# Last tile's first product by seven half products in six single PSUM banks, with its weight sums made earlier

## The chip, the cores and the metric

The kernel runs on one core of a Trainium2 chip. TensorE multiplies matrices, VectorE and ScalarE work on elements, GpSimd does a few set-up steps, SyncE (SP) and ScalarE issue transfers. TensorE writes to PSUM (eight banks of 128 x 512 floats), and the other engines read results from there. The metric is the time of one execution on the device, in microseconds (us).

## The reference, cut to what matters

An attention-like recurrence (rwkv6) gives x, of 3072 tokens by 384; what is changed here lies behind it, in the two-layer network:

```
h = x @ w_in                 # 3072 x 384  by  384 x 2048
g = 0.5 * h * (1 + erf(h / sqrt(2)))
out = g @ w_out              # 3072 x 2048 by 2048 x 384
```

All is float32.

## The kernel before, in words

The tokens are cut into eight tiles of T = 384 (`NX` = 8; two tiles make one sequence). `attention(x, 0)` is a generator that yields in slots; it fills `xT`, tile x's tokens laid out with the model width on the 128 partitions in three parts of 128 (j = 0, 1, 2). `mlp(x)` is a generator for the network of one tile. A main loop steps through `mlp(x - 1)` and at written-out steps (`place`, `place_next`) calls the next slot of `attention(x)`, so the program order on each engine is that of this loop; there is no other scheduler, and each engine runs its instructions in that order. The last tile, `mlp(NX - 1)`, has no attention beside it (L958).

In `mlp`, h is made in 16 strips of 128 of the hidden width (L747 to L754): three products, one for each part j, of 384 columns, accumulated in one PSUM bank `h_ps` (tag "mm", two buffers), and then a Gelu on ScalarE into g. Then g @ w_out: the tile's 384 tokens are three blocks of 128. Blocks 0 and 1 go by seven products of halves (L796 to L838, the method of Strassen and Winograd: the hidden width in two halves of 8 strips, the output width in two halves of `HM` = 192), with sums of g in `s1`, `s2`, `s3` (L763 to L766, on VectorE), sums of w_out in `sums` (`w_sums`, made once), and partial results `p1`, `u2`, `u3`. `product` (L769) issues the eight products of one half. Block 2 of an odd tile is kept (`alone`) and goes with block 2 of the next tile (`waits`, `ends`), but the last tile's block 2 stands alone: 16 plain products of 384 columns (L877 to L893), after the seven, then a copy by VectorE (L891) and a store. Stores are issued on SP's queue (L740). The sums of g are made in the last two of the 16 strips (L758 to L766).

Tile 6, the one before, is an `ends` tile: its steps 16 to 22 are its seven products of g, beside the last slots of `attention(7)`. At step 18 these are the products with v (L595) and the chain of states on VectorE (L610); at step 20 L636 and the fences (L648); at step 21 L674 and the copies of `xT` by ScalarE (L697, L700), with six small transfers for the rest of `xT` (L704). Steps 23 to 27 are five more products, of the kept block pair (L855 to L876), with L856, L859, L862, L864, L867, L870 and L874 as their readers and sums. PSUM is split in a pool `ps`: two single banks of tag "mm", and three pairs of banks of tag "d" for the attention.

The names p, s1 and so on appear in the profile without their numbers; `rkw` is the pair of input buffers (`bufs`), parts of which are used again for `alone`, `p1_alone` and others.

Of the kernel before, what the change touches and what calls it, by code (L numbers as in the profile page):

```python
# [10 lines left out]
F32 = mybir.dt.float32  # L11
# [33 lines left out]
def kernel(  # L45
# [40 lines left out]
    cv = ctx.enter_context(tc.tile_pool(name="cv", bufs=HALFWAY))  # L86
    gp = ctx.enter_context(tc.tile_pool(name="gp", bufs=4))
    ps = ctx.enter_context(tc.tile_pool(name="ps", bufs=1, space=PSUM))
    ctx.enter_context(tc.manual_schedule(engines=None))

    half = [slice(0, 64), slice(64, 128)]
# [94 lines left out]

    def keep_warm(n, elsewhere=False):
        if elsewhere:
            t = ps.tile([128, 2, BANK], F32, name="warm", tag="d", bufs=3)[:, 0]
        else:  # L190
            t = ps.tile([128, BANK], F32, name="warm", tag="mm", bufs=2)
        for _ in range(n):
            nc.tensor.matmul(t, lhsT=zeros[:, 0:128], rhs=zeros, start=True, stop=True)  # L193
# [123 lines left out]
    def attention(x, unit):  # L317
# [78 lines left out]
            yield  # L396

        def products(bs, right, width):
            d = ps.tile([128, 2, BANK], F32, name="d", tag="d", bufs=3)
            n = 0  # L400
            for b in bs:
                for i in range(NI):
                    for g in range(2):
                        for p in range(2):
                            nc.tensor.matmul(d[half[p], g, n * width:(n + 1) * width],  # L405
                                             lhsT=kc[half[g], b, i, p], rhs=right(half[g], b, i, p),
                                             start=True, stop=True)
                    n += 1
            return d[:, :, 0:n * width]
# [64 lines left out]
        def quarters():  # L474
# [26 lines left out]
            yield  # L501
            for h in QUARTERS:
                m, r4, t4, s0, s1, s2 = views(h)
                banks = [ps.tile([128, 2, BANK], F32, name="d", tag="d", bufs=3) for _ in range(0, np_ * NI, 4)]
                if h == FINE:

                    n_b = np_ * NI
                    fine_ps = [banks[-1][:, g, 6 * C:6 * C + FINE * n_b] for g in range(2)]
                    for a in range(FINE):
                        for g in range(2):  # L510
                            nc.tensor.matmul(fine_ps[g][:, a * n_b:], lhsT=places[half[g], a], rhs=fine_sb[half[g], 0:FINE - a, a],  # L511
                                             start=(a == 0), stop=True, skip_group_check=True)
                ds = []
                for n, d in zip(range(0, np_ * NI, 4), banks):
                    for i in range(4):
                        for g in range(2):
                            for p in range(2):
                                nc.tensor.matmul(d[half[p], g, i * 3 * C // 2:(i + 1) * 3 * C // 2],  # L518
                                                 lhsT=kc[half[g], (n + i) // NI, (n + i) % NI, p],
                                                 rhs=rx[half[g], 2 * (n + i) + p], start=True, stop=True)  # L520
                    ds.append(d[:, :, 0:4 * 3 * C // 2].rearrange("p g (n x) -> p g n x", n=4))
                last = h == QUARTERS[-1]

                z = r4[:, :, :, 1:, :].rearrange("p n m b j -> p n m (b j)")
                nc.vector.tensor_mul(z, s0, t4[:, :, :, 0:1].to_broadcast(z.shape))
                if not last:
                    plain(4 * h)
                k4 = k.rearrange("p (n four j) -> p n four j", four=4, j=h)
                z = k4[:, :, 0:2, :].rearrange("p n b j -> p n (b j)")
                t2 = tot[2 * h].rearrange("p (n two) -> p n two", two=2)  # L530
                nc.vector.tensor_mul(z, z, t2[:, :, 1:2].to_broadcast(z.shape))  # L531
                z = k4.rearrange("p n (b two) j -> p n b two j", two=2)[:, :, :, 0, :]
                tz = t4.rearrange("p n m (b two) -> p (n m) b two", two=2)[:, :, :, 1:2]
                nc.vector.tensor_mul(z, z, tz.to_broadcast(z.shape))
                if not last:
                    lay_out(4 * h)
                else:
                    blocks_of_k()
                    yield
                    for move in moves[NC_SP:]:  # L540
                        move_block(nc.scalar, *move)
                for n, d in enumerate(ds):
                    an = at[:, :, 4 * n:4 * n + 4].rearrange("p g n (m x) -> p g n m x", m=m)
                    o = 0
                    for a in range(3):
                        w_q = (3 - a) * C // 4
                        mask = quarter[h][a].rearrange("p (m x) -> p m x", m=m).unsqueeze(1).unsqueeze(1)
                        data = d[:, :, :, o:o + w_q].rearrange("p g n (m x) -> p g n m x", m=m)
                        nc.vector.copy_predicated(out=an[:, :, :, :, (a + 1) * h:], mask=mask.to_broadcast(data.shape), data=data)  # L549
                        o += w_q  # L550
                if h == FINE:
                    mask = fine_mask.rearrange("p (m b) -> p m b", b=FINE).unsqueeze(1)
                    for g in range(2):
                        data = fine_ps[g].rearrange("p (b n) -> p n b", n=n_b)
                        data = data.unsqueeze(2).to_broadcast([128, n_b, C // FINE, FINE])
                        nc.vector.copy_predicated(out=at[:, g].rearrange("p n (m b) -> p n m b", b=FINE),  # L556
                                                  mask=mask.to_broadcast(data.shape), data=data)
                yield
# [4 lines left out]
        if x < 2:  # L563
            kts = []
            for b in range(np_):
                kt_ps = ps.tile([128, 2, BANK], F32, name="kt_ps", tag="d", bufs=3)
                for i in range(NI):
                    o = (i % N3) * 128
                    nc.tensor.transpose(kt_ps[:, i // N3, o:o + 128], k[:, (b * NI + i) * 128:(b * NI + i + 1) * 128], ident)  # L569
# [18 lines left out]

        kvs = []
        for b in range(np_):  # L590
            kv_ps = ps.tile([128, 2, BANK], F32, name="kv_ps", tag="d", bufs=3)
            for i in range(NI):
                for p in range(2):
                    for g in range(2):
                        nc.tensor.matmul(kv_ps[half[g], p, i * D:(i + 1) * D], lhsT=k_t(b, i, p, g),  # L595
                                         rhs=vs(b, i, g)[half[p], 0:D], start=True, stop=True)
            kvs.append(kv_ps[:, :, 0:NI * D].rearrange("p c (q i e) -> p q i c e", q=Q, e=D))
# [27 lines left out]
        def inside():  # L625

            for b in range(np_):
                if split:
                    y = [ps.tile([128, BANK], F32, name="y_ps", tag="mm", bufs=2) for _ in range(2)]
                else:  # L630
                    y_ps = ps.tile([128, 2, BANK], F32, name="y_ps", tag="d", bufs=3)
                    y = [y_ps[:, c] for c in range(2)]
                for i in range(NI):
                    for p in range(2):
# [82 lines left out]
    def w_sums():  # L717
# [3 lines left out]
        for i, (x, y) in enumerate((((0, 1), (0, 0)), ((1, 1), 0), ((1, 1), (0, 1)), ((1, 0), 1))):  # L721
            for k in range(2):
                ks = slice(k * FG, (k + 1) * FG)
                nc.vector.tensor_sub(sums[i][:, ks], w_quarter(*x, k), sums[y][:, ks] if isinstance(y, int) else w_quarter(*y, k))
                yield

    def mlp(x):


# [12 lines left out]
        def new_sums(tag):  # L742
            return cv.tile([128, FG, 128], F32, name="s", tag=tag)

        s1, s2, s3 = [], [], []
        for n, group in enumerate((0, 2, 1, 3) if halves else range(4)):
            gs[group] = gp.tile([128, FG, T], F32, name="g")  # L747
            for f in range(group * FG, (group + 1) * FG):
                h_ps = ps.tile([128, BANK], F32, name="h_ps", tag="mm", bufs=2)[:, 0:T]
# [6 lines left out]
                    nc.scalar.activation(out=alone[:, f], in_=h_ps[:, t:], func=AF.Gelu)  # L756

                if halves and n == 3 and f % FG >= FG - 2:  # L758
                    k = f % FG - FG + 2
                    for s, tag in ((s1, "f"), (s2, "e")):  # L760
                        s.append(new_sums(tag))
                    s3.append(s3_sb[0][:, k * FG:(k + 1) * FG])
                    a00, a10, a11 = (gs[g][:, :, a:a + 128] for g, a in ((k, 0), (k, 128), (k + 2, 128)))  # L763
                    nc.vector.tensor_add(s1[k], a10, a11)  # L764
                    nc.vector.tensor_sub(s2[k], s1[k], a00)
                    nc.vector.tensor_sub(s3[k], a00, a10)  # L766
                yield

        def product(o, lhs, rhs, start=False):  # L769
# [21 lines left out]

        def two_rows():
            return [wk.tile([128, DM], F32, name="o_sb", bufs=2) for _ in range(2)]


        if halves:  # L796
# [54 lines left out]
        elif ends:  # L851
# [22 lines left out]
            nc.vector.tensor_add(o_sb[0][:, 0:HM], o1, u2)  # L874
            store(row0 - T + 256, o_sb[0][:, 0:HM], HM)
            yield  # L876
        else:  # L877

            if halves:
                psum()  # L880
            for blocks in ((2,),) if halves else ((0, 1), (2,)):
                o_ps = [ps.tile([128, BANK], F32, name="o_ps", tag="mm", bufs=2)[:, 0:DM] for _ in blocks]
                for f in range(NF):
                    for i, o in zip(blocks, o_ps):
                        nc.tensor.matmul(o, lhsT=block(i, f // HF, f % HF), rhs=w_out_sb[:, f, :],  # L885
                                         start=(f == 0), stop=(f == NF - 1))
                    if (not halves or f % 4 == 3) and f < NF - 1:
                        yield
                for i, o in zip(blocks, o_ps):
                    o_sb = wk.tile([128, DM], F32, name="o_sb", bufs=2)  # L890
# [39 lines left out]
    for x in range(1, NX):  # L930
# [8 lines left out]
        for step, _ in enumerate(mlp(x - 1)):  # L939
# [12 lines left out]
            while place_next and place_next[0] <= step:  # L952
                place_next.pop(0)
                next(following, None)
        for _ in slots:
            pass
        slots = following
# [62 lines left out]
```

## Time and profile before

| | us |
|---|---|
| median of four runs (607.61 to 608.85) | 607.95 |
| the profiled execution | 607.84 |
| its span, first to last instruction | 605.3 |
| TensorE busy in the span | 589.6 (97%) |
| VectorE busy | 446.7 (74%) |
| ScalarE busy | 173.4 (29%) |
| h of all tiles, 768 records of 384 columns | 254.2 |
| granted clock of TensorE, mean | 1.000 |

The profile's rows give start and length in us, then engine, line of the kernel, operation, what it writes and reads, shape, and how many instructions were merged into the row (x16). PE is TensorE's products, PEld its weight loads, DVE VectorE, ACT ScalarE, SPq the issue of transfers by SP. Brackets give the idle time of the engine before the row, and what ended it. [...]rows of TensorE overlap by some 0.16 us; the distance between starts is what a product takes. The records' granted clock is 1.0 throughout. The chain that ended last is TensorE for 93% of the span.

### The profile page before, as it was taken

The numbers are of one execution on the slowest core, as the hardware profiler recorded it, in microseconds if no ns is written. First come the engines' busy times: TensorE is split into PE (matmuls) and PEld (weight loads), VectorE is DVE, ScalarE is ACT, GpSimd is POOL, SyncE is SP. The second block draws the span as 40 slices with busy tenths as digits, with TensorE's granted clock in tenths as the row PEclk, the third lists the DMA queues.
The fourth block names the chain that finished last, engine by engine and source line by source line (L and its number), as shares of the span: only waits on it lengthen the run. The fifth ranks groups of instructions, "written<-read, shape, count | busy, mean of one in ns | idle before, by whom it ended". The sixth has DMA issues, their size and how long they took to land.

```text
span 605.3 us, 15833 instructions
## 1 busy us (share of the span) xinstructions
PE 589.6 (97%) x6913; PEld 445.0 (74%) x6928; DVE 446.7 (74%) x837; ACT 173.4 (29%) x389; POOL 8.4 (1%) x24
## 2 busy tenths in 40 slices
PE   8769999999999999999999999999999999999997
PEld 4556666656698669986699568986699568995694
DVE  7979999998876978488885988579885988621120
ACT  2346376023222322213222332213222232112200
POOL 3100000000000000000000000000000000000000
PEclk9999999999999999999999999999999999999999
DMA  5767358112041305203042304203052002010001
GB/s 198 233 221 228 107 158 301 34 35 75 15 118 59 92 2 110 73 21 93 1 111 79 92 2 95 86 21 93 2 111 72 8 1 40 23 37 0 1 1 39
DMA packets 50564, 46.70 MB, mean 77 GB/s; under 512 B 31680, under 2 KB 35904, under 8 KB 50496
## 3 DMA queue, kind: packets, MB, share of 16 engines
q1 hardware_dynamic: 33152, 29.31, 15.9%
q10 hardware_dynamic: 17344, 16.39, 10.0%
q8 instruction: 54, 0.88, 0.6%
q14 instruction: 14, 0.11, 0.1%
HBM read 36.24 MB, written 4.72 MB: 68 GB/s over the span
## 4 chain that ended last, share of the span: by engine, by line
PE 93%; DVE 5%; issue 1%; ACT 0%; DVEq 0%
PE h_ps L751 40%; PE o_ps L771 31%; PE o_ps L885 7%; PE d L518 4%; PE d L405 2%; PE kv_ps L595 2%; PE y_ps L674 2%; PE y_ps L636 2%; DVE rkw L440 2%; PE warm L193 1%; DVE a_sb L450 1%; PE d L511 1%; DVE a_sb L416 1%; PE kt_ps L569 0%; DVE e L309 0%
## 5 line engine op out<-in xcount | busy, mean ns | idle before, releaser
L751 PE MATMUL h_ps<-xT,w_in_sb 128*128 128x384 f32 x768 | 254.2, 489 | 0.0
L751 PEld LDWEIGHTS h_ps<-xT,w_in_sb 128*128 128x128 f32 x768 | 144.1, 190 | 97.0 <-ACT xT L681 0.4
L754 ACT ACTIVATE g<-h_ps 128x384 f32<-128x384 f32 (+1 forms) x128 | 57.2, 449 | 196.4 <-PE h_ps L751 196.4
L771 PE MATMUL o_ps<-t,s 128*128 128x192 f32 x480 | 81.9, 329 | 0.0
L771 PEld LDWEIGHTS o_ps<-t,s 128*128 128x128 f32 x480 | 77.8, 190 | 0.7
L549 DVE COPY_PREDICATED a_sb<-quarter,d 128x384 f32<-128x384 uint8 (+2 forms) x108 | 45.1, 439 | 2.5
L885 PE MATMUL o_ps<-w_out_sb,g 128*128 128x384 f32 x128 | 42.7, 490 | 0.0
L771 PE MATMUL o_ps<-w_out_sb,g 128*128 128x192 f32 x224 | 38.7, 326 | 0.0
L771 PEld LDWEIGHTS o_ps<-w_out_sb,g 128*128 128x128 f32 x224 | 37.0, 190 | 1.9
L885 PEld LDWEIGHTS o_ps<-w_out_sb,g 128*128 128x128 f32 x128 | 23.8, 190 | 16.3 <-DVE o_sb L891 0.6
L610 DVE SCALAR_TENSOR_TENSOR st<-st,tot_sb,kv_ps 128x48 f32<-128x48 f32 x160 | 29.0, 259 | 4.1 <-PE kv_ps L595 4.1
L764 DVE TENSOR_TENSOR s<-g 128x512 f32<-128x512 f32 x14 | 9.4, 671 | 29.1 <-ACT g L754 29.1
L771 PE MATMUL o_ps<-w_out_sb,s 128*128 128x192 f32 x160 | 28.3, 330 | 0.0
L405 PEld LDWEIGHTS d<-rkw 64*64 64x64 f32 x1152 | 18.8, 136 | 12.8 <-DVE rkw L440 7.4
L771 PE MATMUL o_ps<-t,g 128*128 128x192 f32 x160 | 27.6, 326 | 0.0
L342 DVE TRANSPOSE_TENSOR_REDUCE rkw<-kx 128x48 f32<-128x1536 f32 (+3 forms) x24 | 26.8, 1157 | 0.2
L518 PEld LDWEIGHTS d<-kx,rkw 64*64 64x64 f32 x1152 | 24.3, 133 | 3.4 <-DVE a_sb L556 1.6
L518 PE MATMUL d<-kx,rkw 64*64 64x96 f32 x1152 | 26.5, 245 | 0.0
L771 PEld LDWEIGHTS o_ps<-t,g 128*128 128x128 f32 x160 | 26.3, 190 | 0.0
L771 PEld LDWEIGHTS o_ps<-w_out_sb,s 128*128 128x128 f32 x160 | 25.9, 190 | 0.4
L405 PE MATMUL d<-rkw 64*64 64x64 f32 (+1 forms) x1152 | 21.3, 223 | 5.1 <-DVE rkw L440 2.9
L531 DVE TENSOR_TENSOR rkw<-rkw,tot_sb 128x768 f32<-128x768 f32 x12 | 11.5, 959 | 17.3 <-PE d L518 17.3
(116 smaller groups left out, 632.9 us busy)
## 6 DMA issues: line engine op xcount, KB each, us to landing
rkw<-in_rkw_dram ACTq DMA_DIRECT2D x45, 256.0 KB, 2.8
raw<-in_w_out_dram SPq DMA_DIRECT2D x8, 768.0 KB, 4.4
out_dram<-o_sb SPq DMA_DIRECT2D x21, 192.0 KB, 1.9
raw<-in_w_in_dram SPq DMA_DIRECT2D x5, 768.0 KB, 5.9
v_in<-in_v_dram ACTq DMA_DIRECT2D x5, 584.0 KB, 3.6
raw<-in_w_in_dram SPq DMA_DIRECT2D x9, 256.0 KB, 3.4
rkw<-in_rkw_dram SPq DMA_DIRECT2D x8, 288.0 KB, 3.4
rkw<-in_rkw_dram SPq DMA_DIRECT2D x9, 256.0 KB, 7.5
```

What stands on the lines that cost most here:

```text
L342: nc.vector.tensor_reduce(out=fine_sb[:, e, 0:n].rearrange("p a n -> p (a n)"), in_=kx[:, o:o + n * n_m].rearrange("p (m j) -> p m j", j=3 ...
L405: nc.tensor.matmul(d[half[p], g, n * width:(n + 1) * width], lhsT=kc[half[g], b, i, p], rhs=right(half[g], b, i, p), start=True, stop=True)
L440: nc.vector.tensor_mul(rk, rk, tt)
L518: nc.tensor.matmul(d[half[p], g, i * 3 * C // 2:(i + 1) * 3 * C // 2], lhsT=kc[half[g], (n + i) // NI, (n + i) % NI, p], rhs=rx[half[g], 2 ...
L549: nc.vector.copy_predicated(out=an[:, :, :, :, (a + 1) * h:], mask=mask.to_broadcast(data.shape), data=data)
L595: nc.tensor.matmul(kv_ps[half[g], p, i * D:(i + 1) * D], lhsT=k_t(b, i, p, g), rhs=vs(b, i, g)[half[p], 0:D], start=True, stop=True)
L610: nc.vector.scalar_tensor_tensor(out=stq[:, q, c], in0=stq[:, q, c - 1] if c else b4[:, q, NC - 1], scalar=totq[:, q, c:c + 1], in1=kvs[q ...
L636: nc.tensor.matmul(y[p][half[g ^ swap(b)], i * C:(i + 1) * C], lhsT=vs(b, i, g)[half[p]], rhs=at[half[p], g, b * NI + i, :], start=(i == 0 ...
L751: nc.tensor.matmul(h_ps, lhsT=w_in_sb[:, f // FI, j, f % FI * 128:(f % FI + 1) * 128], rhs=xT[:, j, :], start=(j == 0), stop=(j == NJ - 1))
L754: nc.scalar.activation(out=gs[group][:, f % FG, 0:t], in_=h_ps[:, 0:t], func=AF.Gelu)
L771: nc.tensor.matmul(o, lhsT=lhs(j), rhs=rhs(j), start=start and j == 0, stop=(j == HF - 1), skip_group_check=True)
L885: nc.tensor.matmul(o, lhsT=block(i, f // HF, f % HF), rhs=w_out_sb[:, f, :], start=(f == 0), stop=(f == NF - 1))
```

## The change: what it does, and the diff

For the last tile, h is made by seven products of halves over the first two parts of the model width (j = 0, 1), the two halves a = 0, 1 of the hidden width (strips f and f + 8), and the two halves b of the tokens (192 each). The third part (j = 2) is added by plain products of 192 columns. So there are eight blocks, one for each f, of 11 products of 192 columns, in six single banks in place of the two: p1 (in b_1), S2 T2 (b_6), S3 T3 (b_7), S1 T1 (b_5), the rest of h00 (b_1 again, added to it), w11 T4 and its third part (b_4), a third part alone (b_0), S4 x11 and a third part (b_5 again, added). VectorE adds them to u2, u3, u5, c21, c22, c12; ScalarE copies p1 and takes four Gelus of 192 columns a block, one from b_1 and three from the sums in SBUF. The Gelu of c12 is issued in the next block behind the copy of p1. In the profile the six banks b_1, b_6, b_7, b_5, b_4, b_0 are named b0 to b5, in that order.

`h_sums` makes the sums of w_in (S1 to S4, eight instructions of 128 x 512) and of xT (T1 to T4, four of 128 x 192) on VectorE, at steps 18, 22 (two parts) and 25 of the tile before, into buffers that are no longer read: parts of `rkw`, `kx`, `tot_sb` and a new `v_in`. The sums of g (`of_g`) are spread over the blocks 4 to 6 and behind the last. The third token block's 16 products go ahead of the seven products of g, with the copy on ScalarE; L891 and its store at the end are gone for the last tile. The pairs of banks get a pool of their own (`pd`), which is closed before the six banks are opened; every other use of tag "d" only changes its pool's name.

```diff
+    pairs_of_banks = ctx.enter_context(ExitStack())
+    pd = pairs_of_banks.enter_context(tc.tile_pool(name="pd", bufs=3, space=PSUM))
...
+    def h_sums():
+        n = DF // 2
+        rest = io.tile([128, v.shape[2]], F32, name="v_in")
+        for z in (bufs[0][:, 0:n], rest[:, 0:n], kx[:, 0:n], bufs[1][:, ALL:ALL + n]):
+            in_s.append(z.rearrange("p (i c) -> p i c", c=WI))
...
+        for i in range(4):
+            for k in range(2):
+                if i == 0:
+                    nc.vector.tensor_add(s(1, k), w(1, 0, k), w(1, 1, k))
+                elif i == 1:
+                    nc.vector.tensor_sub(s(2, k), s(1, k), w(0, 0, k))
+                elif i == 2:
+                    nc.vector.tensor_sub(s(3, k), w(0, 0, k), w(1, 0, k))
+                else:
+                    nc.vector.tensor_sub(s(4, k), w(0, 1, k), s(2, k))
+            if i < 3:
+                yield
...
+        nc.vector.tensor_sub(in_t[0], x01, x00)
+        nc.vector.tensor_sub(in_t[1], x11, in_t[0])
+        nc.vector.tensor_sub(in_t[2], x11, x01)
+        nc.vector.tensor_sub(in_t[3], x10, in_t[1])
+        yield
...
+        def of_g(k):
...
+            nc.vector.tensor_add(s1[k], a10, a11)
+            yield
+            nc.vector.tensor_sub(s2[k], s1[k], a00)
+            yield
+            nc.vector.tensor_sub(s3[k], a00, a10)
+            yield
+
+        def h_halves():
+            pairs_of_banks.close()
+            pb = ctx.enter_context(tc.tile_pool(name="pb", bufs=1, space=PSUM))
+            b_1, b_6, b_7, b_5, b_4, b_0 = (pb.tile([128, BANK], F32, name=f"b{i}")[:, 0:HT] for i in range(6))
...
+            for f in range(HF):
...
+                multiply(b_1, (w(0, 0), x00))
+                nc.scalar.copy(out=p1, in_=b_1)
+                for z in late:
+                    gelu(*z)
+                multiply(b_6, (s(2), in_t[1]))
+                nc.vector.tensor_add(u2, b_6, p1)
+                multiply(b_7, (s(3), in_t[2]))
+                nc.vector.tensor_add(u3, b_7, u2)
+                multiply(b_5, (s(1), in_t[0]))
+                nc.vector.tensor_add(u5, b_5, u3)
+                multiply(b_1, (w(0, 1), x10), (w(0, 2), last[0]), start=False)
+                gelu(0, 0, b_1)
+                multiply(b_4, (w(1, 1), in_t[3]), (w(1, 2), last[0]))
+                nc.vector.tensor_add(c21, b_4, u3)
+                gelu(1, 0, c21)
+                multiply(b_0, (w(1, 2), last[1]))
+                nc.vector.tensor_add(c22, b_0, u5)
+                gelu(1, 1, c22)
+                multiply(b_5, (s(4), x11), (w(0, 2), last[1]), start=False)
+                nc.vector.tensor_add(c12, b_5, u2)
+
+                late = [(0, 1, c12, f)]
+                next(more, None)
+                if f % FG == FG - 1:
+                    more = of_g(k)
+            for z in late:
+                gelu(*z)
+            for _ in more:
+                pass
...
+        final = x == NX - 1
+        if final:
+            h_halves()
+        for n, group in enumerate(() if final else (0, 2, 1, 3) if halves else range(4)):
...
+        if final:
+            o_ps = ps.tile([128, BANK], F32, name="o_ps", tag="mm", bufs=2)[:, 0:DM]
+            order = [f for f in range(NF) if f % HF < HF - 1] + [HF - 1, NF - 1]
+            for n, f in enumerate(order):
+                nc.tensor.matmul(o_ps, lhsT=block(2, f // HF, f % HF), rhs=w_out_sb[:, f, :], start=(n == 0), stop=(n == NF - 1))
+            o_sb = wk.tile([128, DM], F32, name="o_sb", bufs=2)
+            nc.scalar.copy(out=o_sb, in_=o_ps)
+            store(x * T + 256, o_sb)
+            yield
...
+            if x == NX - 1:
+                if step == 18:
+                    more_h = h_sums()
+                for _ in range({18: 1, 22: 2, 25: 1}.get(step, 0)):
+                    next(more_h)
```

In the changed file h's products of the last tile are on L828, the Gelus on L832, VectorE's sums on L840 to L854, the sums of `h_sums` on L752 to L767, `product` on L888, the third block on L917 and L919, and L832, L867 and L891 of before are L960, L995 and L1017 there.

## The prediction

> **What bounds the kernel now.** I read the page first (shares of each engine, the chain that ended last), then the chain by time for the last 106 us, then the timeline of the last tile, then the pauses of VectorE before it.
>
> The chain by time, its end; the columns are start, length (us) and what:
>
> ```profile
> 542.25 30.96 PE h_ps L751 x96
> 573.21 18.20 PE o_ps L771 x112
> 591.41 10.33 PE o_ps L885 x32
> 601.75 0.02 issue
> 601.77 0.56 DVE o_sb L891
> ```
>
> From 542 us on the chain is TensorE alone: h of the last tile, seven products of g, the third token block, and one copy. So time that TensorE needs less here is taken off the end, unless a new wait stands in its place. Each matrix product is two records ("passes"): 16 x 3 products are x96. A pass of 384 columns takes 30.96 / 96 = 322.5 ns.
>
> The timeline of that stretch gives the pass of 192 columns, the time from TensorE to the reader, and each reader's cost:
>
> ```profile
> 573.05 2.76 PE L771 MATMUL o_ps<-w_out_sb,g 128*128 128x192 f32 x16
> 575.49 2.63 PEld L771 LDWEIGHTS o_ps<-t,g 128*128 128x128 f32 x16
> 575.65 2.76 PE L771 MATMUL o_ps<-t,g 128*128 128x192 f32 x16
> 575.85 0.32 ACT L802 COPY p<-o_ps 128x192 f32<-128x192 f32 x1 [2.11 <-PE o_ps L771]
> 583.72 0.36 DVE L811 TENSOR_TENSOR u<-o_ps,p 128x192 f32<-128x192 f32 x1 [7.93 <-PE o_ps L771]
> 591.45 0.36 DVE L832 TENSOR_TENSOR o_sb<-o_ps,u 128x192 f32<-128x192 f32 x1 [1.52 <-PE o_ps L771]
> 601.77 0.56 DVE L891 COPY o_sb<-o_ps 128x384 f32<-128x384 f32 x1 [9.96 <-PE o_ps L885]
> ```
>
> 573.05 to 575.65 is 2.60 us for 16 passes: 162.5 ns each. A weight load starts 0.16 us ahead of its pass (575.49 against 575.65). A reader with one wait starts 0.20 us after the last pass (575.65 to 575.85); L811, which waits for two engines, 0.27 us after (583.45, worked out as 580.85 + 16 x 0.1625, to 583.72).
>
> The timeline of VectorE ahead of the last tile; brackets hold the idle time before:
>
> ```profile
> 518.37 0.35 DVE L811 TENSOR_TENSOR u<-o_ps,p 128x192 f32<-128x192 f32 x1
> 518.64 1.28 DVE L817 TENSOR_TENSOR s<-g,s 128x512 f32<-128x512 f32 x2
> 521.47 0.16 DVE L648 COPY fence<-y_ps 128x2 f32<-128x2 f32 x1 [1.55 <-PE y_ps L636]
> 529.57 1.28 DVE L837 TENSOR_TENSOR s<-s,rkw 128x512 f32<-128x512 f32 x2
> 534.49 0.36 DVE L859 TENSOR_TENSOR u<-o_ps,rkw 128x192 f32<-128x192 f32 x1 [3.64 <-PE o_ps L771]
> 534.77 1.28 DVE L864 TENSOR_TENSOR s<-rkw,s 128x512 f32<-128x512 f32 x2
> 539.69 0.36 DVE L867 TENSOR_TENSOR u<-o_ps,rkw 128x192 f32<-128x192 f32 x1 [3.64 <-PE o_ps L771]
> ```
>
> Three pauses, of 1.55, 3.64 and 3.64 us; a pair of 128x512 sums costs 1.28.
>
> **h by halves: what TensorE saves.** Before: 96 passes x 322.5 ns = 30.96 us. After: 8 blocks x 11 products (seven of halves, four for the third part of the model width) x 2 = 176 passes of 192 columns, x 162.5 ns = 28.60 us. Columns fall to 11/12 only, as the third part isn't shortened, and the fixed part of a pass is paid 80 times more. Gain: 2.36 us, if no pass waits.
>
> Weight loads are what speaks against it: they grow from 96 to 176. The Trainium skill, TensorE: Matmul & The Clock Gate, Part 3 (The mechanism), has loads overlap running matmuls only where their row groups differ; here every load takes all 128 rows. By that rule 80 more loads at columns/1.2 = 107 ns (its LDWEIGHTS section; an estimate) cost 8.5 us, and the change loses 8.5 - 2.36 = 6.2 us (Part 2 of that page leaves room for a background weight buffer, without a figure). The row decides: 16 passes with 16 full loads take 2.60 us, 162.5 ns each, less than one load's own record (190 ns in the groups). The loads hide behind 192 columns too, so I add nothing; I keep "190 ns a pass" as a rival.
>
> **The waits inside a block.** One product is m = 0.325 us, a block 11m = 3.575 us. VectorE has six 192-column sums in it (6 x 0.36 = 2.2 us), ScalarE a copy (0.32) and four Gelus of 192 columns. Those are not in the trace; its Gelus of 128 and 256 columns take 273 and 383 ns, so 273 is the low end, 383 the high end, and I take 328 as between; 0.32 + 4 x 0.33 = 1.6 us. Neither engine is full. What matters is when banks return. From the end T of a block, a released bank being seen by TensorE 0.05 us after VectorE ends (early in the trace VectorE's L440 ends at 20.24, the waiting load starts at 20.29), I need it 0.16 us ahead of the pass, for its load:
> - bank b_5: c12 starts T + 0.20, ends 0.56, seen 0.61; needed 3m - 0.16 = 0.815. Slack 0.20.
> - bank b_1: its first product ends 0.325, ScalarE copies it 0.525 to 0.845 (the Gelu ahead of it, of c22, starts near 0.03 and is done by 0.36, at 383 ns by 0.41), seen 0.90; needed 4m - 0.16 = 1.14. Slack 0.24. ScalarE to TensorE has no such row; at 0.20 in place of 0.05 the slack is 0.09, and at 0 it is 0.29.
> - b_5 again: u2 from 2m + 0.27 = 0.92 to 1.28, u3 to 1.68, u5 to 2.08, seen 2.13; needed 9m - 0.16 = 2.765. Slack 0.63; in three blocks a 128x512 sum of g (0.69, row L764's size) stands ahead of u2, and 0.22 remains.
> - the Gelu of b_1 frees it at about 2.5, needed 3.4.
> The three tight waits hold up the passes queued behind them. My value is no stall. A stall can't gain time. For its high end I let one wait per block be late by a whole load's lead: 8 x 0.16 = 1.3 us.
>
> **Sums of w_in and xT.** The first pair goes behind the state chain and ahead of L811: L811 ends 518.72 + 1.28 = 520.0, and its bank is needed by the product at 522.03; L817 ends 521.20, its readers start at 526.39; the fence at 521.47 still comes first: the pause of 1.55 shrinks to 0.27. The next four (2.56) follow L837, 530.85 to 533.41, ahead of L859 at 534.49. The last two follow L864 (536.05 to 537.33), then four 192-column sums of xT, which wait for its DMAs (issued 527.03 on, 24 KB, 1.9 us to landing) and take 4 x 0.36: to 538.8, ahead of L867 at 539.69. All in pauses: nothing. If this cover were gone, all 6.6 us would fall on VectorE, but TensorE feels only what passes its own next need; the least is 0.9 us (538.8 against 539.69), and past it only L867's bank, needed 2.6 us later.
>
> **Third block ahead of g's products.** The same 32 passes x 322.5 ns = 10.32 us, moved. Its copy goes to ScalarE (0.48 for 128x384 at L700), behind the 2.6 us of the next product before the bank is asked for again. Its store goes to SP first of the last three; SP has nothing else then, and it lands 1.9 us later, near 583.7 (block's end 581.0, copy and issue 0.7), ahead of the copy at 586.4 that needs its row buffer. It also covers the sums of g's second half. Now the last product's reader is L832's sum (0.36) in place of L891's copy (0.56), each 0.20 after the last pass: 0.20 us gained. The last two stores then stand 1.87 us apart (589.96 and 591.83 now), and there each landed in 1.9 us, like the lone last one. Nothing more. The pool of PSUM pairs is closed and six single banks opened: the first product then waits for readers that were done 10 us earlier. Nothing. The order on every engine up to there is unchanged, but for the sums.
>
> **Sum:** 2.36 + 0.20 = 2.56 us. The profiled execution took 607.84 (span 605.3): 605.28 after. Its time is 0.11 below the median of 607.95: 605.39, so I say 605.4.
>
> **Rivals.** 0.2% (1.22 us, about what a measurement here can tell from no change) makes 606.7 to 609.2 "the same".
> - No stall: 605.4. For it: waits are met with 0.2 us to spare, and none of the 192-column products stalls. Chance 0.72.
> - Some stall, up to 0.16 a block: up to 605.4 + 1.3 = 606.7. For it: two slacks of 0.2 rest on single rows, and a satisfied wait that late is not in the trace. Chance 0.14.
> - The wait takes the place of the work: at 0.32 a block TensorE idles 2.56 us, 607.95. It needs c12's way back to take 0.815 + 0.32 = 1.14 in place of 0.61 us. No row is that slow. Chance 0.08.
> - Loads become the bound (slower): in L828's run of unlike banks a pass takes a load's 190 ns: 176 x 0.190 = 33.44, + 2.48 - 0.20 = + 2.28: 610.2. It decides from (30.96 + 0.20) / 176 = 177 ns a pass. Against it stands the 162.5 of L771. Chance 0.06, all on the slower side.
> That it does less than it says is possible at one place: if the sums don't fit the pauses, the first block starts late; that is inside the second case.
>
> So faster 0.86, the same 0.08, slower 0.06. Range: 604.9 (0.5 below for the scatter; the four runs span 607.61 to 608.85) to 606.7, the end of the stalls.
>
> **What would show it.** Right: h of the last tile spans 28.6 us with no idle in its TensorE rows, 176 passes, blocks 3.575 apart; the third block starts near 570.7; the chain ends in L960's sum of 0.36. Wrong: idle before b3 (b_5) or b0 (b_1) named "DVE" or "ACT"; passes over 162.5 ns in a block; L995 or the fences later than now, with TensorE idle ahead of L828; a last store landing later than 1.9 us.

## The result, and the profile after

The changed kernel takes 605.74 us (median of 39 runs, 602.42 to 609.12) where the kernel before, in the runs made beside it, takes 607.77 (58 runs, 604.52 to 611.45). The ratio is 0.9964, with a 95% interval of 0.9953 to 0.9975. Against 607.77 that is 2.2 us gained, 1.5 to 2.9 by the interval; 2.56 us was forecast (a ratio of 0.9958).

Single executions scatter by more than that: the profiled one of the changed kernel took 608.43 us with a span of 606.6, *more* than the profiled one of before. So the profile has to be read from a common mark. The chain by time of the changed kernel, its end (start, length, what):

```profile
546.13 28.60 PE b L828 x176
574.73 10.32 PE o_ps L917 x32
585.05 18.21 PE o_ps L888 x112
603.26 0.02 issue
603.28 0.36 DVE o_sb L960
```

h is 28.60 us where it was 30.96, the third block is the same 10.32, g's products the same, and the end is a sum of 0.36 us, not a copy of 0.56. I call "tail" the time from the first product of the last tile's h to the end of the last VectorE instruction. Before: 542.09 to 602.33, 60.24 us. After: 545.96 to 603.64, 57.68 us. The difference is 2.56 us. All else in this profiled run is that the last tile began 3.87 us later. The timelines show where that came from, in TensorE's rows of before and of after:

```profile
37.42 0.45 PE L595 MATMUL kv_ps<-v_in,kx 64*64 64x48 f32 x17 [1.23 <-issue]
37.70 1.17 PE L674 MATMUL y_ps<-rkw,st 64*64 64x64 f32 x34
45.12 4.11 PE L751 MATMUL h_ps<-xT,w_in_sb 128*128 128x384 f32 x12
```

```profile
40.76 0.45 PE L598 MATMUL kv_ps<-v_in,kx 64*64 64x48 f32 x17 [3.16 <-issue]
41.03 1.95 PE L677 MATMUL y_ps<-rkw,st 64*64 64x64 f32 x34
48.05 4.11 PE L874 MATMUL h_ps<-xT,w_in_sb 128*128 128x384 f32 x12
175.86 1.69 PE L598 MATMUL kv_ps<-v_in,rkw 64*64 64x48 f32 x92 [0.53 <-DMA rkw<-kx]
```

The first h product is 2.93 us later. The stop ahead of the kv row is 3.16 us, not 1.23, and one near 28 us is 1.63, not 0.46 (why, the profile doesn't show). Behind the longer stop TensorE also ran slower: its granted clock was 0.5 from 41.16 to 44.57 us, and the same 34 products took 1.95 us in place of 1.17. From the kv row to the first h product is 7.29 us here and 6.75 in the halves-alone run below, at full clock, so the clock has some 0.5 of the 2.93 us. Another 0.8 us is lost by 173.8 us, where kv waits for transfers, and 0.13 near 312 (times of before). All of it lies in instructions that both kernels have in the same order. From there on the two run 3.87 us apart, to within 0.01, up to the last tile, and in the tails of both the granted clock is 1.0.

The timeline of one block of h (the second; it begins at 549.54):

```profile
549.74 0.36 DVE L854 TENSOR_TENSOR rkw<-b,u 128x192 f32<-128x192 f32 x1 [0.29 <-PE b L828]
549.86 0.49 PE L828 MATMUL b<-tot_sb,v_in 128*128 128x192 f32 x2
550.06 0.32 ACT L836 COPY p<-b 128x192 f32<-128x192 f32 x1 [0.22 <-PE b L828]
550.35 0.35 PEld L828 LDWEIGHTS b<-tot_sb,rkw 128*128 128x128 f32 x2
550.51 0.49 PE L828 MATMUL b<-tot_sb,rkw 128*128 128x192 f32 x2
550.91 0.36 DVE L842 TENSOR_TENSOR u<-b,u 128x192 f32<-128x192 f32 x1
551.37 0.36 DVE L844 TENSOR_TENSOR rkw<-b,u 128x192 f32<-128x192 f32 x1
553.44 0.49 PE L828 MATMUL b<-tot_sb,v_in 128*128 128x192 f32 x2
```

549.86 to 553.44 is one block: 3.58 us, as 22 passes of 162.5 ns. No row of L828 has idle time ahead of it. The old c12 (L854) is done at 550.10, and the load of b_5's next product starts at 550.35: the bank is back 0.25 us early. b_1's copy (L836) is done at 550.38, 0.30 us ahead of the next load for that bank at 550.68. VectorE's pauses of the tile before:

```profile
522.24 1.29 DVE L752 TENSOR_TENSOR rkw<-w_in_sb 128x512 f32<-128x512 f32 x2
523.44 0.35 DVE L939 TENSOR_TENSOR u<-o_ps,p 128x192 f32<-128x192 f32 x1
525.34 0.16 DVE L651 COPY fence<-y_ps 128x2 f32<-128x2 f32 x1 [0.35 <-PE y_ps L639]
538.36 0.36 DVE L987 TENSOR_TENSOR u<-o_ps,rkw 128x192 f32<-128x192 f32 x1 [1.24 <-PE o_ps L888]
541.97 0.35 DVE L767 TENSOR_TENSOR tot_sb<-xT,tot_sb 128x192 f32<-128x192 f32 x1
543.56 0.36 DVE L995 TENSOR_TENSOR u<-o_ps,rkw 128x192 f32<-128x192 f32 x1 [1.24 <-PE o_ps L888]
```

The pauses of 1.55, 3.64 and 3.64 us have shrunk to 0.35, 1.24 and 1.24, and the fence, L987 and L995 start 3.87 us later than their fellows before (521.47, 534.49, 539.69), which is the shift of the whole run and nothing more. So the sums cost TensorE nothing.

### The profile page after: what moved, and what is told of

Its sections match the earlier page's. It is cut to its first block, busy times and chain, and to the rows that moved or that the text cites. A ratio compares the mean times of both kernels' runs of the same rounds, so it can differ in the third digit from the quotient of the medians.

```text
span 606.6 us, 16117 instructions
## 1 busy us (share of the span) xinstructions
PE 589.0 (97%) x6993; PEld 457.1 (75%) x7008; DVE 468.5 (77%) x896; ACT 179.0 (30%) x414; POOL 8.4 (1%) x24
## 4 chain that ended last, share of the span: by engine, by line
PE 70%; DMA 1%; issue 0%; DVE 0%; ACTq 0%
PE o_ps L888 29%; PE h_ps L874 26%; PE b L828 5%; PE d L521 4%; PE o_ps L917 2%; PE kv_ps L598 2%; PE y_ps L639 2%; PE y_ps L677 1%; DMA rkw<-kx 1%; PE d L514 1%; DVE o_sb L960 0%; ACTq L468 0%
## 5 line engine op out<-in xcount | busy, mean ns | idle before, releaser
L874 PE MATMUL h_ps<-xT,w_in_sb 128*128 128x384 f32 x672 | 223.0, 489 | 0.0
L874 PEld LDWEIGHTS h_ps<-xT,w_in_sb 128*128 128x128 f32 x672 | 125.9, 190 | 84.6 <-ACT xT L684 0.4
L877 ACT ACTIVATE g<-h_ps 128x384 f32<-128x384 f32 (+1 forms) x112 | 49.4, 444 | 168.3 <-PE h_ps L874 168.3
L888 PE MATMUL o_ps<-t,s 128*128 128x192 f32 x480 | 81.9, 329 | 0.0
L888 PEld LDWEIGHTS o_ps<-t,s 128*128 128x128 f32 x480 | 77.8, 190 | 0.7
L888 PE MATMUL o_ps<-w_out_sb,g 128*128 128x192 f32 x224 | 38.7, 326 | 0.0
L888 PEld LDWEIGHTS o_ps<-w_out_sb,g 128*128 128x128 f32 x224 | 37.0, 190 | 1.9
L1011 PE MATMUL o_ps<-w_out_sb,g 128*128 128x384 f32 x96 | 32.2, 491 | 0.0
L888 PE MATMUL o_ps<-w_out_sb,s 128*128 128x192 f32 x160 | 28.3, 330 | 0.0
L888 PE MATMUL o_ps<-t,g 128*128 128x192 f32 x160 | 27.6, 326 | 0.0
L1011 PEld LDWEIGHTS o_ps<-w_out_sb,g 128*128 128x128 f32 x96 | 17.7, 190 | 12.3 <-DVE o_sb L1017 0.6
L888 PEld LDWEIGHTS o_ps<-t,g 128*128 128x128 f32 x160 | 26.3, 190 | 0.0
L888 PEld LDWEIGHTS o_ps<-w_out_sb,s 128*128 128x128 f32 x160 | 25.9, 190 | 0.4
L381 DVE TENSOR_TENSOR rkw<-rkw 128x384 f32<-128x384 f32 (+2 forms) x24 | 23.6, 1006 | 0.4
```

The lines of the kernel that those rows point to most:

```text
L381: nc.vector.tensor_mul(z, z, by)
L874: nc.tensor.matmul(h_ps, lhsT=w_in_sb[:, f // FI, j, f % FI * 128:(f % FI + 1) * 128], rhs=xT[:, j, :], start=(j == 0), stop=(j == NJ - 1))
L877: nc.scalar.activation(out=gs[group][:, f % FG, 0:t], in_=h_ps[:, 0:t], func=AF.Gelu)
L888: nc.tensor.matmul(o, lhsT=lhs(j), rhs=rhs(j), start=start and j == 0, stop=(j == HF - 1), skip_group_check=True)
```

## The experiments

As whole runs scatter by some 3 us, each kernel is read by its tail, and the timed ratio stands beside it. Each tail comes from one profile. That this is enough is seen where kernels have stretches in common: h in the kernel before and with the block moved (30.96 us both), h by halves in the changed kernel and alone (28.60), and the whole tail of the changed kernel and of the last run (57.68). The granted clock is 1.0 in every tail but that of the late sums.

| kernel | last tile's h starts | tail, us | expected | ratio to before, 95% interval |
|---|---|---|---|---|
| before | 542.09 | 60.24 | | |
| changed | 545.96 | 57.68 | 57.68 | 0.9964 (0.9953 to 0.9975) |
| third block first, alone | 543.19 | 60.04 | 60.04 | 1.0007 (0.9988 to 1.0026) |
| halves alone | 542.38 | 57.88 | 57.88 | 0.9966 (0.9950 to 0.9982) |
| sums at the head of the last tile | 543.98 | 66.06 | 63.6 | 1.0098 (1.0064 to 1.0132) |
| b_5 returned 0.6 later | 541.50 | 59.58 | 60.2 | 0.9987 (0.9973 to 1.0001) |
| five banks | 543.58 | 64.74 | 64.2 | 1.0076 (1.0048 to 1.0104) |
| before, 128 columns | 543.37 | 61.44 | 60.7 | 1.0021 (1.0003 to 1.0039) |
| before, 64 columns | 542.41 | 93.60 | 90.7 | one run, 640.85 us |
| last store in two | 541.81 | 57.68 | 57.68 | 0.9942 (0.9918 to 0.9966) |

**Each part alone.** The third block moved in the kernel before, with nothing else:

```diff
+        final = x == NX - 1
+        if final:
+            o_ps = ps.tile([128, BANK], F32, name="o_ps", tag="mm", bufs=2)[:, 0:DM]
...
+            nc.scalar.copy(out=o_sb, in_=o_ps)
+            store(x * T + 256, o_sb)
...
-        else:
+        elif not final:
```

> The kernel before, with only the third token block's products of the last tile put ahead of the seven products of g (copy on ScalarE). Measure: the tail, from the first product of the last tile's h to the end of the last VectorE instruction; it is 60.24 us before and 57.68 us in the changed kernel. My theory (the gain is 2.36 us of columns in h and 0.20 us of a shorter last reader): tail 60.04, 0.2 us less than before, too little for the timed runs to show. Rival (the order of the blocks carries a larger part, because g's sums and banks come back in time): tail well below 60.0, at most 58 if it carries most.

And the changed kernel with that block back at the end:

```diff
-        if final:
-            o_ps = ps.tile([128, BANK], F32, name="o_ps", tag="mm", bufs=2)[:, 0:DM]
...
-            store(x * T + 256, o_sb)
...
-        elif not final:
-            for blocks in (0, 1), (2,):
+        else:
+            if halves:
+                psum()
+            for blocks in ((2,),) if halves else ((0, 1), (2,)):
```

> The changed kernel with the third token block back behind the products of g: h by halves alone. My theory: tail 60.24 - 2.36 = 57.88 us, about 0.4% faster than before. Rival (the block ahead covers the last sums of g and the last Gelu, and without it TensorE waits for them): tail above 57.9 with TensorE idle ahead of the products of g, up to 1 us more.

The chain by time, of the block alone and then of the halves alone:

```profile
543.35 30.96 PE h_ps L751 x96
574.31 10.32 PE o_ps L801 x32
602.87 0.36 DVE o_sb L844
```

```profile
542.54 28.60 PE b L828 x176
571.14 18.20 PE o_ps L888 x112
599.70 0.56 DVE o_sb L1008
```

Tails 60.04 and 57.88: 0.20 us and 2.36 us, and they add up to the 2.56. The order of blocks hides nothing that h by halves needs: behind h without it, g's products start at once. The timed ratios agree, though 0.2 us is far below what they can tell.

**The sums without their cover.** All twelve are made at the head of the last tile (the edit also hands `xT` to `h_sums`):

```diff
-            if x == NX - 1:
-                if step == 18:
-                    more_h = h_sums()
-                for _ in range({18: 1, 22: 2, 25: 1}.get(step, 0)):
-                    next(more_h)
...
         if final:
+            for _ in h_sums(xT):
+                pass
             h_halves()
```

> The changed kernel with all twelve sums of w_in and xT made in one run on VectorE at the head of the last tile, not in VectorE's pauses of the tile before. My theory (the pauses are what makes them free): the second product of the first block waits for VectorE until eight sums (4.8 us) and two of xT (0.7) are done, from 0.56 us on: about 5.9 us of TensorE idle, tail 57.68 + 5.9 = 63.6 us, 3.3 us over before, so slower by about 0.5%. Rival (where the sums are made does not matter, as VectorE has little to do there): tail 57.7.

The tail is 66.06, 2.5 us more than expected, and 8.38 more than in the changed kernel. The stall is as worked out: the second product's row, of the timeline, starts at 550.07, and without a stall would have been at 544.30 (543.98 + 2 x 0.1625):

```profile
550.07 1.01 PE L827 MATMUL b<-tot_sb,v_in 128*128 128x192 f32 x2 [5.60 <-DVE tot_sb L764]
```

That is 5.77 us. The rest is in the table of stretches (stretch, length, then busy us and instructions of TensorE, its loads, VectorE, ScalarE and GpSimd, granted clock, DMA share, GB/s):

```profile
546.00:548.00 2.00, 0.00 (x0) 0.00 (x0) 2.00 (x4) 0.00 (x0) 0.00 (x0) 1.00 0.00 0
548.00:550.00 2.00, 0.00 (x0) 0.00 (x0) 1.97 (x6) 0.00 (x0) 0.00 (x0) 0.60 0.00 0
550.00:552.00 2.00, 1.93 (x6) 1.93 (x7) 1.15 (x5) 0.00 (x0) 0.00 (x0) 0.50 0.00 0
554.00:556.00 2.00, 2.00 (x10) 2.00 (x10) 0.72 (x2) 0.48 (x3) 0.00 (x0) 0.70 0.00 0
556.00:558.00 2.00, 2.00 (x14) 2.00 (x13) 1.06 (x3) 0.83 (x3) 0.00 (x0) 1.00 0.01 4
```

The granted clock falls to one half near 548.4 (0.60 over two us is 1.6 of them at 0.5), 3.9 us into the idle time of 5.60, and is back near 555.2. From 550.07 that is 5.1 us at half speed, 2.6 us lost: 5.77 + 2.6 = 8.4. The Trainium skill, TensorE: Matmul & The Clock Gate, Part 1 (What's actually happening), has the clock halved after an idle window of some 3.4 us. Here the stall is longer than that and agrees. But shorter stops in these traces were followed by half clock too: 3.16 us in the changed kernel's profile (above), and 2.33 us near 36 us in this run's. One of 2.61 (five banks) and one of 2.88 us (128 columns) were not, so length alone doesn't decide. What the fall costs is plain: nearly half of what the stall does. So uncovered sums make the change 5.8 us worse than no change.

**A bank returned late.** Two more VectorE reads of b_5's bank in each block, with results that nobody uses:

```diff
                 nc.vector.tensor_add(c12, b_5, u2)
+                for i in range(2):
+                    nc.vector.tensor_add(dumps[i], b_5, u2)
```

> The changed kernel with two more 192-column VectorE sums that read b_5's bank behind c12 in each block (results not used), so that the bank returns 0.56 us later. My theory (slack 0.20 us, as the wait must be met 0.16 us ahead for the weight load): 0.36 us of stall in seven blocks, 2.5 us, tail 60.2 us, all of the change's gain. Rival a (the load does not wait, only the product does; slack 0.36): 0.2 us in seven blocks, tail 59.1. Rival b (TensorE runs ahead or around the wait): tail 57.7.

The timeline of this kernel, one block:

```profile
549.13 0.36 DVE L855 TENSOR_TENSOR rkw<-b,u 128x192 f32<-128x192 f32 x1 [0.29 <-PE b L829]
549.40 0.61 DVE L857 TENSOR_TENSOR rkw<-b,u 128x192 f32<-128x192 f32 x2
549.58 0.49 PE L829 MATMUL b<-tot_sb,kx 128*128 128x192 f32 x2
550.07 0.30 PEld L829 LDWEIGHTS b<-tot_sb,rkw 128*128 128x128 f32 x2 [0.30 <-DVE rkw L857]
550.07 0.59 PE L829 MATMUL b<-tot_sb,rkw 128*128 128x192 f32 x2
550.50 0.81 PE L829 MATMUL b<-xT,w_in_sb 128*128 128x192 f32 x4
```

VectorE ends at 550.01 and the load starts 0.06 us later, at 550.07, about as assumed (0.05). The next product starts at 550.50, so the waiting one took effect 0.325 before, at 550.175: 0.105 us after its load began. Without the wait it would have begun at 549.905 (549.58 + 0.325). The stall is 0.27 us, in seven blocks 1.9: tail 59.58. The two reads end 0.52 us after c12 (549.49), not 0.56; with that, my theory gives 0.32 a block and rival a 0.16. The measured 0.27 lies between: the load does wait and is exposed, but it costs 0.105 us, not the 0.16 us by which it normally runs ahead. That TensorE runs around the wait is refuted.

**Five banks.** b_7's product in b_6's bank:

```diff
-            b_1, b_6, b_7, b_5, b_4, b_0 = (pb.tile([128, BANK], F32, name=f"b{i}")[:, 0:HT] for i in range(6))
+            b_1, b_6, b_5, b_4, b_0 = (pb.tile([128, BANK], F32, name=f"b{i}")[:, 0:HT] for i in range(5))
+            b_7 = b_6
```

> The changed kernel with b_7's product in b_6's bank, five banks in place of six: that product must wait until VectorE has read b_6 (u2). My theory (a wait that is not met 0.16 us ahead stalls TensorE by what it is late): u2 ends 1.27 us into the block, seen 1.31, the pass starts at 1.47 in place of 0.65: 0.82 us in eight blocks, 6.6 us, tail 64.2, slower than before by 0.6%. Rival (banks are not what makes it free): tail 57.7.

```profile
549.21 0.36 DVE L841 TENSOR_TENSOR u<-b,p 128x192 f32<-128x192 f32 x1 [0.70 <-ACT g L833]
552.98 0.49 PE L829 MATMUL b<-tot_sb,v_in 128*128 128x192 f32 x2
553.56 0.36 DVE L841 TENSOR_TENSOR u<-b,p 128x192 f32<-128x192 f32 x1 [0.35 <-ACT p L837]
553.97 0.30 PEld L829 LDWEIGHTS b<-tot_sb,kx 128*128 128x128 f32 x2 [0.80 <-DVE u L841]
554.40 0.49 PE L829 MATMUL b<-tot_sb,rkw 128*128 128x192 f32 x2
```

In this block, the third, the product of b_7 takes effect at 554.40 - 0.325 = 554.08 in place of 552.98 + 0.325 = 553.31: 0.77 late, where 0.82 was worked out. So it is in blocks 3 to 5. In blocks 6 to 8 the sum of g ahead of u2 makes it 0.93 (blocks begin 4.51 apart). The first block loses 0.80, and the second 1.12: there (first row) u2 starts later, and the profile names a Gelu that ended ahead of it (why only there, it doesn't show). The eight add up to 7.06 us, by which the tail of 64.74 exceeds the changed kernel's: one bank fewer takes the whole gain and 4.5 us more.

**How narrow may a product be?** The kernel before, with its plain h of the last tile in narrower products of the same sum:

```diff
+                n_w = 128 if x == NX - 1 else T
                 for j in range(NJ):
-                    nc.tensor.matmul(h_ps, lhsT=w_in_sb[:, f // FI, j, f % FI * 128:(f % FI + 1) * 128], rhs=xT[:, j, :],
-                                     start=(j == 0), stop=(j == NJ - 1))
+                    for c in range(0, T, n_w):
+                        nc.tensor.matmul(h_ps[:, c:c + n_w], lhsT=w_in_sb[:, f // FI, j, f % FI * 128:(f % FI + 1) * 128],
+                                         rhs=xT[:, j, c:c + n_w], start=(j == 0 and c == 0), stop=(j == NJ - 1), skip_group_check=True)
```

> The kernel before, with the last tile's plain h in products of 128 columns in place of 384: the same columns, three times the weight loads (288 passes). By the two rows a pass costs 0.833 ns a column and 2.5 ns. My theory (loads hide behind the columns): 288 x 109.2 ns = 31.4 us of h, tail 60.7. Rival (a load takes its record of 190 ns and sets the pass once columns are short): 54.7 us, tail 84. Rival (a load takes the 162.5 ns that the 192-column pass shows): 46.8 us, tail 76.

The same with `n_w` = 64:

> As the run with 128 columns, with 64: 576 passes. If loads hide at any width: 576 x 55.8 ns = 32.2 us of h, tail 61.5. If a load takes what the Trainium skill's page on TensorE gives for 128 columns, 107 ns (an estimate): 61.4 us, tail 90.7. If it takes 162.5 ns: 93.6 us. I expect the second: the width at which halving stops being free lies between 64 and 128 columns.

The chain by time, of 128 columns and then of 64:

```profile
543.54 32.16 PE h_ps L753 x288
```

```profile
542.57 64.26 PE h_ps L753 x576
```

And the loads of the latter, in a timeline:

```profile
549.89 3.21 PEld L753 LDWEIGHTS h_ps<-xT,w_in_sb 128*128 128x128 f32 x28
```

32.16 / 288 = 111.7 ns and 64.26 / 576 = 111.6 ns: the same pass at half the columns. So here something else than columns sets the pace, at 111.6 ns. I put it down to the load, the one thing in a pass that did not shrink: the 28 loads shown follow each other by the same pace ((3.21 - 0.19) / 27 = 111.9 ns), with no gap. That issuing an instruction takes so long is ruled out, as small products of 64 x 64 come much faster in the same traces (kv above: 17 records in 0.45 us). A pass then takes the longer of 111.6 ns and 2.5 ns + 0.833 ns a column (109.2 ns at 128, 55.8 at 64). The two would meet at (111.6 - 2.5) / 0.833 = 131 columns, an estimate, as no width between 128 and 192 was run. So at 128 columns loads no longer hide: my theory's h of 31.4 us was 0.7 short, and the meeting point is not between 64 and 128, where I expected it. Both rivals of the wider run (a load of 190 or of 162.5 ns) are refuted; the load's record of 190 ns is not what it costs. The 107 ns that the narrower run took for the load came out 5 ns short. That its tail, 93.60 us, looks like the third case's 93.6 is chance: there 93.6 is h alone, and h took 64.26.

**The last store in two.** The changed kernel with the last rows' left half stored as soon as it is there:

```diff
             nc.scalar.copy(out=o_sb[0][:, 0:HM], in_=o1)
+            if final:
+                store(row0, o_sb[0][:, 0:HM])
...
             nc.vector.tensor_add(o_sb[0][:, HM:], o1, u2)
-            store(row0, o_sb[0])
+            if final:
+                store(row0, o_sb[0][:, HM:], HM)
+            else:
+                store(row0, o_sb[0])
```

> The changed kernel with the last store cut in two: the left half of the last rows is stored as soon as it is there, so that the last store is 96 KB, not 192 KB. Both kernels' 96 KB stores land in 1.6 us (median), the 192 KB ones in 1.9. My theory: tail to VectorE's last end unchanged (57.68), and the stretch from there to the end 2.97 - 0.3 = 2.67 us, total 2.9 us below before. Rival (landing is a fixed cost at this size, or the two small stores get in each other's way): 2.97 us or more.

SP's own waits, of the changed kernel and then of this one (us in total, times, longest):

```profile
SPq L1148 <- DMA out_dram<-o_sb: 1.5, 1, 1.5
```

```profile
SPq L1153 <- DMA out_dram<-o_sb: 1.2, 1, 1.2
```

The program's last wait is 0.3 us shorter, and from VectorE's last end to the end of the span it is 602.1 - 599.49 = 2.6 us in place of 606.6 - 603.64 = 3.0 (2.9 to 3.0 in all nine other profiles). The median is 603.95 us, and its ratio to before is 0.9942 (0.9918 to 0.9966): faster than before. Against the changed kernel the traces show the 0.3 us, and the timed runs can't tell them apart (the intervals overlap).

## Why the prediction was right, point by point

- *Columns in h, 2.36 us:* 96 passes of 322.5 ns became 176 of 162.5 ns, and with the halves alone the tail fell by 2.36.
- *Loads hide behind 192 columns:* yes, as the trace of before said. By the rule of separate row groups, cited in the prediction, the change would have lost 6.2 us; measured, it gains 2.36 there, with every load on all 128 rows. The rival priced a load by its record, 190 ns; two widths show 111.6 ns. The room is not large: 192 columns are 1.5 times the width where, by the estimate above, loads take over.
- *Waits met with 0.2 us to spare:* b_5's bank came back 0.25 us ahead of the load, as worked out (0.20 behind the 0.05 for TensorE to see it), and b_1's 0.30 ahead (0.29 worked out in the same way). The working was off in two terms: a late load costs 0.105 us, not 0.16, and u3 and u5, each of which needs the sum before it, start at 1.37 and 1.83 us into the block, not at 1.32 and 1.72. Neither used up the slack. How fast TensorE sees a bank that ScalarE returns was not measured: no wait of that kind became late.
- *Sums in the pauses, nothing:* right, with the least cover 0.35 us at the fence (0.27 worked out) and 1.24 at L995 (0.9). What the cover is worth was told too small in the run without it: I counted the stall only, and this stall brought the halved clock as well.
- *Third block ahead, 0.20 us:* right, and as much as the shorter last reader gives (0.56 to 0.36).
- *No change elsewhere:* right for the instructions; but the scatter of one execution is wider than the four runs I had (607.61 to 608.85) let me think. In ten profiles the last tile's h begins anywhere from 541.50 to 545.96 us. I took 0.5 us below for it. So 605.74 against 605.4 is no failed step that could be found: the difference of 0.3 us is inside the interval of the ratio.

## What to carry to other kernels

Halving a float32 product pays by its columns only while a pass stays above the load: here down to some 131 columns, so a second level of halving, at 96, would by this estimate be bound by loads. Every saved product is paid for with sums and with banks that must come back, so count for each bank when its reader ends and when its next load starts; one bank fewer, or sums made a few microseconds late, cost about three times the gain (7.06 and 8.38 us against 2.56). And where whole runs scatter by more than the effect, compare the traces from a common instruction near the change: the tail gave 0.20 us cleanly where 14 timed runs could not tell its sign.

## What the runs showed of the hardware that was not expected

- A pass with a full weight load of float32 takes 111.6 to 111.7 ns however short its columns (128 and 64 alike), while the load's record is 190 ns long; behind a late wait 0.105 us of the load is exposed.
- Idle for 5.6 us, TensorE lost half of its granted clock 3.9 us into the idle time, and had it back 5.1 us after it began to work again: 6.8 us of half clock. After a stop of 2.33 us it also lasted 6.8 us, and after one of 3.16 us 3.4 us; there the fall came 1.5 and 0.4 us after TensorE had begun again.
- In ten profiles the first h product begins at 44.04 to 48.05 us, and from there to the last tile's h it takes 497.0 to 499.2 us, though TensorE's instructions there are the same. The two that were compared, before and changed, keep step to 0.01 us from some 316 us on.
